# Rebuilding the opening of a one-core adaLN + attention + MLP kernel: larger loads, c turned on TensorE, one tile's LayerNorm on ScalarE, wide warm-up matmuls

## Chip, cores, metric

One core of a Trainium2 chip. The metric is device time in microseconds (us) of one execution; the span in a profile is some 1.7 us shorter. TensorE is PE in the profile (its weight loads PEld), VectorE is DVE, ScalarE is ACT, GpSimd is POOL, SyncE is SP. Most transfers are issued from SP.

## The reference, cut to what matters

```python
x = A_x                                            # 2048 x 512, bf16
mod = silu(c) @ w_mod                              # six rows of 512: sa, ca, ga, sb, cb, gb
h = layernorm(x) * (1 + ca) + sa
x = x + ga * attention(h, k_cache[-512:], v_cache[-512:], wq, wo)   # 32 heads, 8 groups, Dh 128
h = layernorm(x) * (1 + cb) + sb
x = x + gb * (relu(h @ w1) @ w2)                   # 512 -> 1792 -> 512
```

Nothing of attention can start before the first 512 rows are normalised, two of the six modulation rows are there, and both are joined in `hT`. That is the opening.

## The kernel before

Work goes in units of one head by 512 rows, 128 in all; "head n" below is unit n of these. Per unit PE does Q, scores (S), scores times v (psO) and four of the output projection's matmuls (psW), ACT the exp, DVE the division, and SP a transposing transfer that turns the head's result into `oT`. The MLP's weights lie where w_mod was and are loaded in the middle. Cuts are marked.

```python
def load_w1():                                     # w2 in the same way
    for i in range(2):
        f0, f1 = i * FC // 2, (i + 1) * FC // 2
        dma(w1_sb[:, :, f0 * P:f1 * P], w1v[:, :, f0 * P:f1 * P], f"w1{i}", writes=R_w1[f0:f1] + R_wm)
def warm(n):
    for i in range(n):
        mm(bank[WBK][:, :P], ident[:, :], ident[:, :], True, True, [R_ident], [WBK], i == n - 1)
def pv_mms(u):
    # ... psO matmuls, reciprocal and product on DVE into o_sb ...
    dma(oT[u % NOT][:, :, :], o_sb[u % NOS][:, :, :]..., transpose=True)          # on SP
def enqueue_wo(b, j):                              # four of these after each head's psO
    # ... mm(bank[WBK], oT[slot][:, tl, :], wo_sb[:, h, :], ...) ...

# opening
dma(c_col[:, :], c[0].rearrange("(c p) -> p c", p=P), "c", writes=[R_c], eng=ACT)
for t in range(TPB):
    dma(x_sb[:, t, :], xv[:, t, :], f"xa{t}", writes=[R_x[t]], eng=ACT if t % 2 else SP)
load_wm(1); load_wm(0); load_wq(0, 2); load_k(0); load_v(0); load_wq(2, 2)
# ... constants on POOL, exp table on ACT ...
warm(48)
ln_stat(0); ln_stat(1); silu(); ln_stat(2); ln_rstd(0, 0, 3); ln_stat(3); ln_rstd(0, 3, 4)
for tl in range(3):
    ln_norm(tl); ln_tposes(tl, [0, 2])
for f in mod_cols_mm(0, QBK): f()
ln_norm(3); ln_tposes(3, [0, 2]); mod_cols_evac(0, QBK)
ln_mod_ps([0, 2], hT[0], R_hT[0], 1)
# ... Q of two heads, then the loop over units ...
add(60, load_w1)                                   # at unit 60 and unit 64
add(64, load_w2)
```

Both halves of a weight claim all of `R_wm`, so SP issues the second half only when the first has landed (in the changed kernel w2's first half lands at 239.19 us and the second is issued at 239.20).

Of the kernel before, what the change touches and what calls it, by code (L numbers as in the profile page):

```python
# [7 lines left out]
ACTF = mybir.ActivationFunctionType  # L8
ALU = mybir.AluOpType
AX = mybir.AxisListType  # L10
BF = mybir.dt.bfloat16
F32 = mybir.dt.float32
# [1185 lines left out]
def build_fast(nc, es, top, A_x, A_k_cache, A_v_cache, A_wq, A_wo, B_x, B_w1, B_w2, c, w_mod, out, flag):  # L1198
    P = 128
    _, Sq, D = A_x.shape  # L1200
# [6 lines left out]
    QB = 512  # L1207
    NB = Sq // QB
    TPB = QB // P
    NT = Sq // P  # L1210
    DC = D // P
# [3 lines left out]
    scale = float(Dh) ** -0.5  # L1215
    eps = 1e-5
# [10 lines left out]
    def T(name, shape, dt=BF):  # L1227
        return es.enter_context(nc.sbuf_tensor(name, shape, dt))

    x_sb = T("x", [P, NT, D])  # L1230
# [11 lines left out]
    oT = [T(f"oT{i}", [P, TPB, P]) for i in range(NOT)]  # L1242
    acc = T("acc", [P, TPB, D], F32)
    wmw = T("wmw", [P, max(6 * DC * D, DC * F + FC * D)])
    wm = [wmw[:, i * DC * D:(i + 1) * DC * D].rearrange("p (c n) -> p c n", c=DC) for i in range(6)]
    w1_sb = wmw[:, 0:DC * F].rearrange("p (c f) -> p c f", c=DC)
    w2_sb = wmw[:, DC * F:DC * F + FC * D].rearrange("p (f d) -> p f d", f=FC)
    xn = T("xn", [P, TPB, D])
# [3 lines left out]
    yo = [PT[1][:, i, :] for i in range(NY)]  # L1252
    ident = T("ident", [P, P])
    ones = T("ones", [P, P])
    c_col = T("c_col", [P, DC])
    sc_bf = T("sc_bf", [P, DC])
    sc_rep = T("sc_rep", [P, DC, P])
    tmp = T("tmp", [P, DC], F32)
# [4 lines left out]
    mv = T("mv", [P, NT, 2], F32)  # L1263
    rstd = T("rstd", [P, NT], F32)
    cst = T("cst", [P, 4], F32)
# [9 lines left out]
    bank = [s_ps[0][:, 0, :], s_ps[0][:, 1, :], s_ps[1][:, 0, :], s_ps[1][:, 1, :], q_ps[:, :],  # L1275
            o_ps[:, 0:2, :].rearrange("p a b -> p (a b)"), o_ps[:, 2:4, :].rearrange("p a b -> p (a b)"), w_ps[:, :]]
    QBK, WBK = 4, 7

    sem = lambda name: top.enter_context(nc.semaphore(name))
    kb = KB(nc)  # L1280
    PE = kb.stream("pe", sem("s_pe"))
    ACT = kb.stream("act", sem("s_act"))
    DVE = kb.stream("dve", sem("s_dve"))
    POOL = kb.stream("pool", sem("s_pool"))
    SP = kb.stream("sp", sem("s_sp"))
# [6 lines left out]
    def dma(out_ap, in_ap, key, reads=(), writes=(), transpose=False, eng=None):  # L1292
        k = dsem(key)
        if transpose:
            return kb.op(SP, lambda e: e.dma_start_transpose(out_ap, in_ap), reads=reads, writes=writes, dma_sem=k)
        return kb.op(eng or SP, lambda e: e.dma_start(out_ap, in_ap), reads=reads, writes=writes, dma_sem=k)  # L1296

    RL = lambda name, n: [Res(f"{name}{i}") for i in range(n)]
    R_x, R_wq, R_wo = RL("x", NT), RL("wq", H), RL("wo", NPASS)
# [3 lines left out]
    R_acc, R_wm, R_w1, R_w2 = RL("acc", TPB), RL("wm", 6), RL("w1", FC), RL("w2", FC)  # L1303
    R_xn, R_xnT = RL("xn", TPB), Res("xnT")
    R_yt, R_yo = RL("yt", NY), RL("yo", NY)
    R_b = RL("bank", 8)
    R_ident, R_ones, R_c, R_sc, R_screp, R_tmp, R_cst = (Res(n) for n in ("ident", "ones", "c", "sc", "screp", "tmp", "cst"))
    R_moda, R_modb, R_ga, R_gb = Res("moda"), Res("modb"), Res("ga"), Res("gb")
    R_st, R_mv, R_rstd = RL("st", NT), RL("mv", NT), RL("rstd", NT)
    R_rinv, R_vmax, R_chk, R_good, R_flag = Res("rinv"), Res("vmax"), Res("chk"), Res("good"), Res("flag")  # L1310
    R_h1 = [RL(f"h1_{i}_", FC) for i in range(2)]

    xv = A_x[0].rearrange("(p t) d -> p t d", p=P)
# [10 lines left out]
    def load_wq(h0, n, eng=None):  # L1324
        dma(wq_sb[:, :, h0 * Dh:(h0 + n) * Dh], wqv[:, :, h0 * Dh:(h0 + n) * Dh], f"wq{h0}", writes=R_wq[h0:h0 + n], eng=eng)

    def load_k(g):
        dma(kT_sb[:, g, :], A_k_cache[0][g, Sk - W:, :], f"k{g}", writes=[R_kT[g]], transpose=True)
# [1 line left out]
    def load_v(g, eng=None):  # L1330
        dma(v_sb[:, g, :, 0:Dh], A_v_cache[0][g, Sk - W:, :].rearrange("(k p) d -> p k d", p=P), f"v{g}", writes=[R_v[g]], eng=eng)

    def load_wm(sl, eng=None):
        dma(wm[sl], w_mod[:, sl * D:(sl + 1) * D].rearrange("(c p) n -> p c n", p=P), f"wm{sl}", writes=[R_wm[sl]], eng=eng)

    def load_wo(j):
        dma(wo_sb[:, j * HQ:(j + 1) * HQ, :], wov[:, j * HQ:(j + 1) * HQ, :], f"wo{j}", writes=[R_wo[j]])
# [11 lines left out]
    def mm(out_ap, lhsT, rhs, start, stop, reads, bk, signal):  # L1349
        kb.op(PE, lambda e: e.matmul(out_ap, lhsT, rhs, start=start, stop=stop), reads=reads, group_writes=[R_b[k] for k in bk], signal=signal)  # L1350
# [3 lines left out]

    def warm(n):
        for i in range(n):
            mm(bank[WBK][:, :P], ident[:, :], ident[:, :], True, True, [R_ident], [WBK], i == n - 1)

    def ln_stat(t):
        kb.op(DVE, lambda e: e.bn_stats(st[:, t, :], x_sb[:, t, :]), reads=[R_x[t]], writes=[R_st[t]])  # L1360
        kb.op(DVE, lambda e: e.bn_aggr(mv[:, t, :], st[:, t, :]), reads=[R_st[t]], writes=[R_mv[t]])  # L1361

    def ln_rstd(b, lo=0, hi=TPB):
        sl = slice(b * TPB + lo, b * TPB + hi)
        kb.op(DVE, lambda e: e.tensor_scalar(rstd[:, sl], mv[:, sl, 1], eps, None, op0=ALU.add), reads=R_mv[sl], writes=R_rstd[sl])  # L1365
        kb.op(POOL, lambda e: e.tensor_tensor(rstd[:, sl], rstd[:, sl], cst[:, 0:1].to_broadcast([P, hi - lo]), op=ALU.pow),  # L1366
              reads=R_rstd[sl] + [R_cst], writes=R_rstd[sl])

    def ln_norm(t):
        b, tl = t // TPB, t % TPB  # L1370
        kb.op(DVE, lambda e: e.tensor_scalar(xn[:, tl, :], x_sb[:, t, :], mv[:, t, 0:1], rstd[:, t:t + 1], op0=ALU.subtract, op1=ALU.mult),  # L1371
              reads=[R_x[t], R_mv[t], R_rstd[t]], writes=[R_xn[tl]])
# [10 lines left out]
    def ln_tposes(tl, bks):  # L1383
        for cc in range(DC):
            bk = bks[cc // 2]
            o = (cc % 2) * 512 + tl * P
            tpose(bank[bk].bitcast(BF)[:, o:o + P], xn[:, tl, cc * P:(cc + 1) * P], [R_xn[tl]], [bk], cc == DC - 1)
# [15 lines left out]
    CC_ORDER = (0, 2, 1, 3)  # L1403
    QA = 2

    def silu():
        kb.op(ACT, lambda e: e.activation(tmp[:, :], c_col[:, :], ACTF.Exp, scale=-1.0), reads=[R_c], writes=[R_tmp])
        kb.op(DVE, lambda e: e.tensor_scalar(tmp[:, :], tmp[:, :], 1.0, None, op0=ALU.add), reads=[R_tmp], writes=[R_tmp])
        kb.op(DVE, lambda e: e.reciprocal(tmp[:, :], tmp[:, :]), reads=[R_tmp], writes=[R_tmp])
        kb.op(DVE, lambda e: e.tensor_tensor(sc_bf[:, :], c_col[:, :], tmp[:, :], op=ALU.mult), reads=[R_tmp, R_c], writes=[R_sc])  # L1410

    def mod_cols_mm(which, bk):
        fs = []
        for idx, sl in enumerate((0, 1) if which == 0 else (3, 4)):
            for c2 in range(DC):
                for cc in range(DC):
                    last = idx == 1 and c2 == DC - 1 and cc == DC - 1
                    fs.append(lambda sl=sl, c2=c2, cc=cc, col=idx * DC + c2, last=last: mm(
                        bank[bk][:, col:col + 1], wm[sl][:, cc, c2 * P:(c2 + 1) * P], sc_bf[:, cc:cc + 1],
                        cc == 0, cc == DC - 1, [R_sc, R_wm[sl]], [bk], last))  # L1420
        return fs

    def mod_cols_evac(which, bk):
        mo, r = which * 2 * DC, (R_moda, R_modb)[which]
        kb.op(DVE, lambda e: e.tensor_copy(modc[:, mo:mo + DC], bank[bk][:, :DC]), reads=[R_b[bk]], writes=[r])
        kb.op(DVE, lambda e: e.tensor_scalar(modc[:, mo + DC:mo + 2 * DC], bank[bk][:, DC:2 * DC], 1.0, None, op0=ALU.add), reads=[R_b[bk]], writes=[r])
# [100 lines left out]
            add(s0 + TPB + 5 + cc // 2, lambda cc=cc: ln_mod_sb(cc, dst, r, which))  # L1527


    dma(c_col[:, :], c[0].rearrange("(c p) -> p c", p=P), "c", writes=[R_c], eng=ACT)  # L1530
    for t in range(TPB):
        dma(x_sb[:, t, :], xv[:, t, :], f"xa{t}", writes=[R_x[t]], eng=ACT if t % 2 else SP)
    load_wm(1)
    load_wm(0)
    load_wq(0, 2)
    load_k(0)
    load_v(0)
    load_wq(2, 2)
    kb.op(POOL, lambda e: e.memset(ones[:, :], 1.0), writes=[R_ones])
    kb.op(POOL, lambda e: e.affine_select(ident[:, :], ones[:, :], pattern=[[1, P]], compare_op=ALU.is_equal, fill=0.0,  # L1540
                                          base=0, channel_multiplier=-1), reads=[R_ones], writes=[R_ident])
    kb.op(POOL, lambda e: e.memset(cst[:, 0:1], -0.5), writes=[R_cst])
    kb.op(POOL, lambda e: e.memset(v_sb[:, :, :, P:VW], 1.0), writes=[R_v1])
    kb.op(ACT, lambda e: e.activation(cst[:, 2:3], cst[:, 0:1], ACTF.Exp), reads=[R_cst], writes=[Res("dummy")])
    warm(48)
    ln_stat(0)
    ln_stat(1)
    silu()
    ln_stat(2)
    ln_rstd(0, 0, 3)  # L1550
    ln_stat(3)
    ln_rstd(0, 3, 4)
    for tl in range(3):
        ln_norm(tl)
        ln_tposes(tl, [0, 2])
    for f in mod_cols_mm(0, QBK):
        f()
    ln_norm(3)
    ln_tposes(3, [0, 2])
    mod_cols_evac(0, QBK)  # L1560
    ln_mod_ps([0, 2], hT[0], R_hT[0], 1)
    load_wq(R, R)
    load_k(1)
# [8 lines left out]
    for g in range(G):  # L1572
        for i, op in enumerate((ALU.max, ALU.min)):
            add(max(R * g, 3), lambda g=g, i=i, op=op: kb.op(DVE, lambda e: e.tensor_reduce(vmax[:, i, g:g + 1], v_sb[:, g, :, 0:Dh], axis=AX.XY, op=op),
                                                             reads=[R_v[g]], writes=[R_vmax]))
# [221 lines left out]
```

## Time and profile before

| | before |
|---|---|
| time, three runs | 569.95 to 571.03, median 570.52 us |
| span of the profiled run | 568.2 us |
| PE busy | 553.0 us, 97% |
| half clock | about 9.4 to 16.2 us |
| first score matmul | 16.26 us |

A number such as 16.26 is a start in the timeline, from the start of the span.

### The profile page before, as it was taken

Reading aid. Unit: us, or ns where it says so; the run is one execution under the profiler, and the core shown is the slowest. Engines: PE = TensorE matmul, PEld = TensorE weight load, DVE = VectorE, ACT = ScalarE, POOL = GpSimd, SP = SyncE. Lnnn points to the kernel's source line nnn. Section 1 sums busy time; section 2 is a strip of 40 time slices with the busy share of each in tenths; the row PEclk is TensorE's granted clock in tenths of the full one; section 3 lists DMA queues with packets and bytes.
Section 4 is the critical chain, followed back from the end, with each engine's and each line's share of the span. In section 5 each row is a group of like instructions: output and inputs, shape, how many; then the busy total and the mean of one; then the engine's idle time right before and its main releaser. Section 6 shows DMA issues by size and latency. Waiting matters only on the chain.

```text
span 568.2 us, 9662 instructions
## 1 busy us (share of the span) xinstructions
PE 553.0 (97%) x4094; PEld 318.7 (56%) x4169; DVE 242.9 (43%) x532; ACT 347.3 (61%) x445; POOL 38.7 (7%) x41
## 2 busy tenths in 40 slices
PE   6999999999999999989999999999999999999997
PEld 5565555666655555546666555555555654444443
DVE  4344465533334655323336553333354438322133
ACT  2876666666666666656666666666666654432500
POOL 1000000002300000023000000330000000000000
PEclk8999999999999999999999999999999999999999
DMA  8795768331231145742321432121114220210001
GB/s 227 202 192 119 179 131 171 81 74 38 39 76 38 38 81 124 167 108 42 75 39 37 75 75 39 38 38 38 38 37 67 47 39 1 38 38 22 22 28 47
DMA packets 111620, 42.67 MB, mean 75 GB/s; under 512 B 94032, under 2 KB 111184, under 8 KB 111568
## 3 DMA queue, kind: packets, MB, share of 16 engines
q1 hardware_dynamic: 110752, 41.70, 34.4%
q8 instruction: 34, 0.56, 0.4%
q10 hardware_dynamic: 816, 0.26, 0.2%
q14 instruction: 18, 0.15, 0.1%
HBM read 18.35 MB, written 2.10 MB: 36 GB/s over the span
## 4 chain that ended last, share of the span: by engine, by line
PE 96%; DMA 2%; DVE 1%; issue 1%; ACTq 0%
PE psS L1350 28%; PE psO L1350 26%; PE psQ L1350 23%; PE psW L1350 19%; DMA oT<-o 1%; DMA x<-in_A_x_dram 1%; DVE st L1360 0%; PE psS L1353 0%; DVE hT L1397 0%; DVE PT L1631 0%; DVE PT L1632 0%; DVE mv L1361 0%; DVE o L1475 0%; ACTq L1296 0%; DVE xn L1371 0%
## 5 line engine op out<-in xcount | busy, mean ns | idle before, releaser
L1464 ACT ACTIVATE PT<-psS 128x1024 bf16<-128x1024 f32 x256 | 262.8, 1028 | 131.7 <-PE psS L1350 131.7
L1350 PE MATMUL psS<-qT,kT 128*128 128x512 bf16 x509 | 151.2, 379 | 0.2
L1350 PEld LDWEIGHTS psO<-v,PT 128*128 128x128 bf16 x2048 | 126.6, 98 | 30.2
L1350 PE MATMUL psO<-v,PT 128*128 128x129 bf16 x2048 | 137.0, 220 | 0.0
L1350 PE MATMUL psQ<-hT,wq 128*128 128x512 bf16 x507 | 130.8, 381 | 1.1 <-DVE hT L1397 1.1
L1474 DVE RECIPROCAL rinv<-psO 128x4 f32<-128x4 f32 x128 | 23.3, 182 | 234.5 <-PE psO L1350 234.5
L1350 PE MATMUL psW<-wo,oT 128*128 128x512 bf16 x451 | 118.1, 379 | 5.3 <-DMA oT<-o 2.1
L1475 DVE TENSOR_TENSOR o<-psO,rinv 128x512 bf16<-128x512 f32 x128 | 88.5, 691 | 4.7 <-DVE rinv L1474 0.3
L1350 PEld LDWEIGHTS psQ<-hT,wq 128*128 128x128 bf16 x508 | 49.7, 98 | 61.1 <-issue 1.0
L1350 PEld LDWEIGHTS psS<-qT,kT 128*128 128x128 bf16 x512 | 49.7, 98 | 59.5 <-ACT PT L1464 0.7
L1456 ACT ACTIVATE qT<-psQ 128x512 bf16<-128x512 f32 x127 | 75.4, 593 | 1.2 <-PE psQ L1350 1.2
L1350 PEld LDWEIGHTS psW<-wo,oT 128*128 128x128 bf16 x512 | 44.9, 98 | 35.4 <-DMA oT<-o 2.6
L1620 ACT ACTIVATE wq<-psS 128x512 bf16<-128x512 f32 x56 | 33.4, 597 | 49.2 <-PE psS L1350 49.2
L1497 DVE TENSOR_TENSOR acc<-psW,acc 128x512 f32<-128x512 f32 x48 | 33.1, 690 | 9.0 <-PE psW L1350 9.0
L1350 PE MATMUL psO<-wmw,wq 128*128 128x512 bf16 x136 | 31.0, 379 | 0.3
L1366 POOL TENSOR_TENSOR rstd<-rstd,cst 128x4 f32<-128x4 f32 (+2 forms) x9 | 8.6, 961 | 273.5 <-DVE rstd L1365 273.4
L1500 POOL TENSOR_TENSOR acc<-acc,gaf 128x512 f32<-128x512 f32 x12 | 15.2, 1268 | 171.0 <-DVE acc L1497 171.0
L1350 PE MATMUL psS<-h2T,wmw 128*128 128x512 bf16 x110 | 25.2, 379 | 0.1
L1350 PE MATMUL psS<-hT,wmw 128*128 128x512 bf16 x110 | 24.4, 379 | 0.1
L1631 DVE TENSOR_TENSOR PT<-psO,gbf 128x512 f32<-128x512 f32 x10 | 6.9, 691 | 40.2 <-PE psO L1350 40.2
L1360 DVE BATCH_NORM_STATS2 st<-x 128x6 f32<-128x512 bf16 x32 | 21.7, 680 | 4.6 <-DMA x<-in_A_x_dram 4.6
L1350 PEld LDWEIGHTS psO<-wmw,wq 128*128 128x128 bf16 x140 | 13.7, 98 | 16.5
(60 smaller groups left out, 168.8 us busy)
## 6 DMA issues: line engine op xcount, KB each, us to landing
wo<-in_A_wo_dram SPq DMA_DIRECT2D x4, 1024.0 KB, 5.9
wq<-in_A_wq_dram SPq DMA_DIRECT2D x7, 512.0 KB, 5.8
wmw<-in_B_w_dram SPq DMA_DIRECT2D x4, 896.0 KB, 5.2
wmw<-in_w_mod_dram SPq DMA_DIRECT2D x6, 512.0 KB, 5.2
oT<-o SPq DMA_TRANSPOSE x128, 2.4
out_dram<-PT SPq DMA_DIRECT2D x16, 128.0 KB, 1.7
x<-in_A_x_dram SPq DMA_DIRECT2D x3, 512.0 KB, 4.2
v<-in_A_v_cache_dram SPq DMA_DIRECT2D x8, 128.0 KB, 4.6
```

The source lines that it names most:

```text
L1350: kb.op(PE, lambda e: e.matmul(out_ap, lhsT, rhs, start=start, stop=stop), reads=reads, group_writes=[R_b[k] for k in bk], signal=signal)
L1360: kb.op(DVE, lambda e: e.bn_stats(st[:, t, :], x_sb[:, t, :]), reads=[R_x[t]], writes=[R_st[t]])
L1366: kb.op(POOL, lambda e: e.tensor_tensor(rstd[:, sl], rstd[:, sl], cst[:, 0:1].to_broadcast([P, hi - lo]), op=ALU.pow), reads=R_rstd[sl] + ...
L1456: kb.op(ACT, lambda e: e.activation(qT[u % NQT][:, :], bank[bk], ACTF.Copy), reads=[R_b[bk]], writes=[R_qT[u % NQT]])
L1464: kb.op(ACT, lambda e: e.activation(PT[u % NPT][:, pr * 2:pr * 2 + 2, :], s_ps[pr][:, :, :], ACTF.Exp, scale=scale), reads=[R_b[pr * 2], R ...
L1474: kb.op(DVE, lambda e: e.reciprocal(rinv[:, u, :], o_ps[:, :, P]), reads=[R_b[5], R_b[6]], writes=[R_rinv])
L1475: kb.op(DVE, lambda e: e.tensor_tensor(o_sb[u % NOS][:, :, :], o_ps[:, :, 0:P], rinv[:, u, :].unsqueeze(2).to_broadcast([P, TPB, P]), op=A ...
L1497: kb.op(DVE, lambda e: e.tensor_tensor(acc[:, tl, :], bank[WBK], acc[:, tl, :], op=ALU.add), reads=[R_b[WBK], R_acc[tl]], writes=[R_acc[tl]])
L1500: kb.op(eng, lambda e: e.tensor_tensor(acc[:, tl, :], acc[:, tl, :], gaf[:, :], op=ALU.mult), reads=[R_acc[tl], R_ga], writes=[R_acc[tl]])
L1620: kb.op(ACT, lambda e: e.activation(h1T[b % 2][:, fc, :], bank[bk], ACTF.Relu), reads=[R_b[bk]], writes=[R_h1[b % 2][fc]], pre=all_events( ...
L1631: kb.op(DVE, lambda e: e.tensor_tensor(yt[i], bank[bk], gbf[:, :], op=ALU.mult), reads=[R_b[bk], R_gb], writes=[R_yt[i]], pre=pt_done if c ...
```

## The change

The intent: shorten the time to the first score, and keep PE's clock up on the way. The diff, cut to its core:

```diff
-    wm = [... one transfer for each of slices 0 and 1 ...]
+    # slices 0 and 1 lie side by side, two transfers of 2 KB rows, each half of the contraction
-            mm(bank[WBK][:, :P], ident[:, :], ident[:, :], True, True, [R_ident], ...)
+            mm(bank[WBK], ones[:, :], ones[:, 0:1].to_broadcast([P, QB]), True, True, [R_ones], ...)
-    dma(c_col[:, :], c[0].rearrange("(c p) -> p c", p=P), "c", ..., eng=ACT)
-    for t in range(TPB):
-        dma(x_sb[:, t, :], xv[:, t, :], f"xa{t}", ..., eng=ACT if t % 2 else SP)
+    dma(c_row[:, :], c[0].rearrange("(c p) -> c p", p=P), "c", ..., eng=ACT)
+    for i in range(2):
+        dma(x_sb[:, 2 * i:2 * i + 2, :], xv[:, 2 * i:2 * i + 2, :], f"xa{i}", ..., eng=ACT if i else SP)
-    warm(48)
+    warm(5); silu_exp(5)          # c transposed on PE, exp read from PSUM
+    warm(14)
+    # tile 3 on ACT: Copy with sum, mean, Square with sum, variance, later the normalising Identity
-    ln_stat(0); ln_stat(1); silu(); ln_stat(2); ...; ln_stat(3); ...
+    ln_stat(0); ln_stat(1); rstd(0:2); ln_stat(2); rstd(2:4); silu_mul(5); ln_norm(0..2)
-    # transposes of tiles 0 to 2, all modulation columns, transposes of tile 3
+    # half the columns, tile 0, the other half, then tiles 1, 2, 3 followed by warm(1), warm(2), warm(3)
```

Nothing after the first Q matmul is touched.

More of the change, by code (lines that the diff above doesn't have):

```diff
@@ L1244, in build_fast @@
     wmw = T("wmw", [P, max(6 * DC * D, DC * F + FC * D)])
-    wm = [wmw[:, i * DC * D:(i + 1) * DC * D].rearrange("p (c n) -> p c n", c=DC) for i in range(6)]
+    wm01 = wmw[:, 0:2 * DC * D].rearrange("p (c n) -> p c n", c=DC)
+    wm = [wm01[:, :, 0:D], wm01[:, :, D:2 * D]] + [wmw[:, i * DC * D:(i + 1) * DC * D].rearrange("p (c n) -> p c n", c=DC) for i in range(2, 6)]
     w1_sb = wmw[:, 0:DC * F].rearrange("p (c f) -> p c f", c=DC)
@@ L1254, in build_fast @@
     ones = T("ones", [P, P])
-    c_col = T("c_col", [P, DC])
+    c_row = T("c_row", [DC, P])
+    s3 = T("s3", [P, 4], F32)
     sc_bf = T("sc_bf", [P, DC])
@@ L1309, in build_fast @@
     R_st, R_mv, R_rstd = RL("st", NT), RL("mv", NT), RL("rstd", NT)
+    R_s3, R_eps = Res("s3"), Res("eps")
     R_rinv, R_vmax, R_chk, R_good, R_flag = Res("rinv"), Res("vmax"), Res("chk"), Res("good"), Res("flag")
@@ L1331, in load_v, with load_wm, load_wm01, wm_res @@
         dma(v_sb[:, g, :, 0:Dh], A_v_cache[0][g, Sk - W:, :].rearrange("(k p) d -> p k d", p=P), f"v{g}", writes=[R_v[g]], eng=eng)
-    def load_wm(sl, eng=None):
-        dma(wm[sl], w_mod[:, sl * D:(sl + 1) * D].rearrange("(c p) n -> p c n", p=P), f"wm{sl}", writes=[R_wm[sl]], eng=eng)
+    def load_wm(sl):
+        dma(wm[sl], w_mod[:, sl * D:(sl + 1) * D].rearrange("(c p) n -> p c n", p=P), f"wm{sl}", writes=[R_wm[sl]])
+    wm01v = w_mod[:, 0:2 * D].rearrange("(c p) n -> p c n", p=P)
+    def load_wm01(i):
+        c0, c1 = i * DC // 2, (i + 1) * DC // 2
+        dma(wm01[:, c0:c1, :], wm01v[:, c0:c1, :], f"wm{i}", writes=[R_wm[i]])
+    def wm_res(sl, cc):
+        return R_wm[cc // (DC // 2)] if sl < 2 else R_wm[sl]
     def load_wo(j):
@@ L1356, in warm @@
         for i in range(n):
-            mm(bank[WBK][:, :P], ident[:, :], ident[:, :], True, True, [R_ident], [WBK], i == n - 1)
+            mm(bank[WBK], ones[:, :], ones[:, 0:1].to_broadcast([P, QB]), True, True, [R_ones], [WBK], i == n - 1)
     def ln_stat(t):
@@ L1404, in build_fast, with silu_exp, silu_mul @@
     QA = 2
-    def silu():
-        kb.op(ACT, lambda e: e.activation(tmp[:, :], c_col[:, :], ACTF.Exp, scale=-1.0), reads=[R_c], writes=[R_tmp])
+    def silu_exp(bk):
+        cT = bank[bk].bitcast(BF)[:, 0:DC]
+        kb.op(PE, lambda e: e.transpose(cT, c_row[:, :], ident[0:DC, 0:DC]), reads=[R_c, R_ident], group_writes=[R_b[bk]])
+        kb.op(ACT, lambda e: e.activation(tmp[:, :], cT, ACTF.Exp, scale=-1.0), reads=[R_b[bk]], writes=[R_tmp])
+    def silu_mul(bk):
+        cT = bank[bk].bitcast(BF)[:, 0:DC]
         kb.op(DVE, lambda e: e.tensor_scalar(tmp[:, :], tmp[:, :], 1.0, None, op0=ALU.add), reads=[R_tmp], writes=[R_tmp])
         kb.op(DVE, lambda e: e.reciprocal(tmp[:, :], tmp[:, :]), reads=[R_tmp], writes=[R_tmp])
-        kb.op(DVE, lambda e: e.tensor_tensor(sc_bf[:, :], c_col[:, :], tmp[:, :], op=ALU.mult), reads=[R_tmp, R_c], writes=[R_sc])
+        kb.op(DVE, lambda e: e.tensor_tensor(sc_bf[:, :], cT, tmp[:, :], op=ALU.mult), reads=[R_tmp, R_b[bk]], writes=[R_sc])
     def mod_cols_mm(which, bk):
@@ L1419, in mod_cols_mm @@
                         bank[bk][:, col:col + 1], wm[sl][:, cc, c2 * P:(c2 + 1) * P], sc_bf[:, cc:cc + 1],
-                        cc == 0, cc == DC - 1, [R_sc, R_wm[sl]], [bk], last))
+                        cc == 0, cc == DC - 1, [R_sc, wm_res(sl, cc)], [bk], last))
         return fs
@@ L1527, in add_ln @@
             add(s0 + TPB + 5 + cc // 2, lambda cc=cc: ln_mod_sb(cc, dst, r, which))
-    dma(c_col[:, :], c[0].rearrange("(c p) -> p c", p=P), "c", writes=[R_c], eng=ACT)
-    for t in range(TPB):
-        dma(x_sb[:, t, :], xv[:, t, :], f"xa{t}", writes=[R_x[t]], eng=ACT if t % 2 else SP)
-    load_wm(1)
-    load_wm(0)
+    dma(c_row[:, :], c[0].rearrange("(c p) -> c p", p=P), "c", writes=[R_c], eng=ACT)
+    for i in range(2):
+        dma(x_sb[:, 2 * i:2 * i + 2, :], xv[:, 2 * i:2 * i + 2, :], f"xa{i}", writes=R_x[2 * i:2 * i + 2], eng=ACT if i else SP)
@@ L1535, in build_fast @@
+    load_wm01(0)
+    load_wm01(1)
     load_wq(0, 2)
+    load_wq(2, 2)
     load_k(0)
     load_v(0)
-    load_wq(2, 2)
     kb.op(POOL, lambda e: e.memset(ones[:, :], 1.0), writes=[R_ones])
+    kb.op(POOL, lambda e: e.memset(cst[:, 0:1], -0.5), writes=[R_cst])
     kb.op(POOL, lambda e: e.affine_select(ident[:, :], ones[:, :], pattern=[[1, P]], compare_op=ALU.is_equal, fill=0.0,
                                           base=0, channel_multiplier=-1), reads=[R_ones], writes=[R_ident])
-    kb.op(POOL, lambda e: e.memset(cst[:, 0:1], -0.5), writes=[R_cst])
+    kb.op(POOL, lambda e: e.memset(cst[:, 1:2], eps), writes=[R_eps])
@@ L1543, in build_fast @@
     kb.op(POOL, lambda e: e.memset(v_sb[:, :, :, P:VW], 1.0), writes=[R_v1])
     kb.op(ACT, lambda e: e.activation(cst[:, 2:3], cst[:, 0:1], ACTF.Exp), reads=[R_cst], writes=[Res("dummy")])
-    warm(48)
+    warm(5)
+    silu_exp(5)
+    warm(14)
+    t3 = TPB - 1
+    kb.op(ACT, lambda e: e.activation(xn[:, t3, :], x_sb[:, t3, :], ACTF.Copy, accum_out=s3[:, 0:1]), reads=[R_x[t3]], writes=[R_xn[t3], R_s3])
+    kb.op(ACT, lambda e: e.activation(s3[:, 1:2], s3[:, 0:1], ACTF.Copy, scale=-1.0 / D), reads=[R_s3], writes=[R_s3])
@@ new lines, in build_fast, with rstd_add @@
+    kb.op(ACT, lambda e: e.activation(xn[:, t3, :], x_sb[:, t3, :], ACTF.Square, bias=s3[:, 1:2], accum_out=s3[:, 2:3]), reads=[R_x[t3], R_s3], writes=[R_xn[t3], R_s3])
+    kb.op(ACT, lambda e: e.activation(rstd[:, t3:t3 + 1], s3[:, 2:3], ACTF.Identity, scale=1.0 / D, bias=cst[:, 1:2]), reads=[R_s3, R_eps], writes=[R_rstd[t3]])
+    def rstd_add(lo, hi):
+        kb.op(DVE, lambda e: e.tensor_scalar(rstd[:, lo:hi], mv[:, lo:hi, 1], eps, None, op0=ALU.add), reads=R_mv[lo:hi], writes=R_rstd[lo:hi])
@@ L1546, in build_fast, with rstd_pow @@
+    def rstd_pow(lo, hi):
+        kb.op(POOL, lambda e: e.tensor_tensor(rstd[:, lo:hi], rstd[:, lo:hi], cst[:, 0:1].to_broadcast([P, hi - lo]), op=ALU.pow),
+              reads=R_rstd[lo:hi] + [R_cst], writes=R_rstd[lo:hi])
     ln_stat(0)
     ln_stat(1)
-    silu()
+    rstd_add(0, 2)
+    rstd_pow(0, 2)
     ln_stat(2)
-    ln_rstd(0, 0, 3)
-    ln_stat(3)
-    ln_rstd(0, 3, 4)
+    rstd_add(2, 3)
+    rstd_pow(2, 4)
+    silu_mul(5)
     for tl in range(3):
         ln_norm(tl)
-        ln_tposes(tl, [0, 2])
@@ L1556, in build_fast @@
-    for f in mod_cols_mm(0, QBK):
-        f()
-    ln_norm(3)
-    ln_tposes(3, [0, 2])
-    mod_cols_evac(0, QBK)
+    kb.op(ACT, lambda e: e.activation(s3[:, 3:4], s3[:, 1:2], ACTF.Copy, scale=rstd[:, t3:t3 + 1]), reads=[R_s3, R_rstd[t3]], writes=[R_s3])
+    kb.op(ACT, lambda e: e.activation(xn[:, t3, :], x_sb[:, t3, :], ACTF.Identity, scale=rstd[:, t3:t3 + 1], bias=s3[:, 3:4]),
+          reads=[R_x[t3], R_rstd[t3], R_s3], writes=[R_xn[t3]])
+    fs = mod_cols_mm(0, QBK)
+    for f in fs[:len(fs) // 2]:
+        f()
@@ L1561, in build_fast @@
+    ln_tposes(0, [0, 2])
+    for f in fs[len(fs) // 2:]:
+        f()
+    mod_cols_evac(0, QBK)
+    for tl in range(1, TPB):
+        ln_tposes(tl, [0, 2])
+        warm(tl)
     ln_mod_ps([0, 2], hT[0], R_hT[0], 1)
```

## The prediction

> **What bounds the kernel now.** I read the page first: the shares of the engines, then the line of the granted clock.
>
> ```profile
> span 568.2 us, 9662 instructions
> PE 553.0 (97%) x4094; PEld 318.7 (56%) x4169; DVE 242.9 (43%) x532; ACT 347.3 (61%) x445; POOL 38.7 (7%) x41
> ...
> PEclk8999999999999999999999999999999999999999
> ...
> PE 96%; DMA 2%; DVE 1%; issue 1%; ACTq 0%
> ```
>
> TensorE is busy for 97% of the span and makes up 96% of the chain that ended last. The change touches only what runs before attention. So it can win only what PE loses in the opening: the one slice (14 us each) whose PE digit is 6 and whose clock digit is 8. Everything later is PE at full clock, and I expect it to move earlier as a block.
>
> Next I cut the opening into stretches by what PE does, and read busy time and granted clock in each (columns: window, length, busy us and number of instructions for PE, PEld, DVE, ACT and POOL, clock, DMA share, GB/s).
>
> ```profile
> 1.40:6.43 5.03, 5.02 (x48) 4.85 (x48) 1.72 (x5) 1.69 (x3) 0.24 (x1) 1.00 0.64 183
> 6.43:9.40 2.97, 0.00 (x0) 0.00 (x0) 2.76 (x12) 0.00 (x0) 1.24 (x2) 1.00 1.22 342
> 9.40:12.20 2.80, 2.74 (x48) 2.48 (x48) 1.25 (x5) 0.00 (x0) 0.32 (x1) 0.50 1.22 239
> 12.20:16.26 4.06, 2.98 (x8) 1.24 (x10) 1.33 (x3) 2.04 (x3) 0.00 (x0) 0.50 1.15 326
> 16.26:20.00 3.74, 3.74 (x20) 1.44 (x19) 0.00 (x0) 3.54 (x5) 0.00 (x0) 1.00 1.07 287
> ```
>
> The 48 warm-up matmuls end at 6.43, PE idles 2.97 us, and from about 9.4 to 16.2 the clock is half: transposes, modulation columns and the first eight Q matmuls all run cold. (The 1.00 of the first row is before the first recorded change at 5.97; 48 matmuls of 128 columns in 5.02 us are 105 ns each, so they ran cold as well.)
>
> Then the chain that ended last, and the timeline, for why PE idled (start, length, what).
>
> ```profile
> 1.27 4.25 DMA x<-in_A_x_dram
> ...
> 5.55 0.70 DVE st L1360
> ...
> 8.94 0.42 DVE xn L1371
> 9.37 0.05 issue
> 9.41 1.46 PE psS L1353 x12
> 10.87 0.83 PE psQ L1350 x32
> 11.71 0.46 PE psS L1353 x4
> 12.17 0.04 issue
> 12.21 1.01 DVE hT L1397 x2
> 13.22 0.06 issue
> 13.28 1.49 PE psQ L1350 x3
> 14.77 1.65 PE psO L1350 x4
> ```
>
> VectorE waited until 5.53 for the second tile of x, then did three tiles' statistics and the silu in one queue; PE got its first xn at 9.41. The packets of the trace say why that tile was late: it sits on the ACT queue behind c, which came in as 512 packets of 2 bytes from 2.19 to 3.95 us; x's packets on that queue start only at 4.06. Meanwhile SP's 1 KB packets crawl too: from 2.5 to 4.0 the rate is 67 GB/s, from 6 to 8 it is 380. Landings from issue times plus time to landing: x tiles 3.3, 5.5, 4.75 and 7.0; c 4.4; w_mod's two slices 7.8 and 9.3; first wq 10.1; first kT 10.8; first v 11.3.
>
> [...]its clock changes lie 3.413 and 6.827 us apart (5.97, 9.38, 16.2). [...]the window 9.4 to 12.8, mostly transposes and one-column matmuls, did not lift the clock, and the next one of wide matmuls did. [...]the trace has 597 ns for the 512-column copy and about 720 ns with two pointers[...].
>
> **The change part by part.**
> *c as 4 rows.* 512 packets become 4. By the first packet's 2.19 and the half microsecond or so from x's last packet to its landing, I put c at about 2.9 instead of 4.4, and some 1.7 us of crawling DMA is gone. It costs one small PE transpose.
> *2 KB rows.* x comes in two transfers of 256 KB, w_mod's first 1 MB in two halves by contraction rows. At 380 GB/s from about 2 us: first x pair about 3.5, second about 4.5, w_mod (1.57 MB in all) about 6.7 instead of 9.3, wq 7.5 and 9, kT and v about 10. I take all these off the path.
> *VectorE queue.* Three statistics (0.69 + 0.18 each) instead of four, silu after them. From 3.5: two tiles to 5.3, rstd add 5.5, third tile and its add 6.6, silu (0.14 + 0.18 + 0.16 and gaps) 7.15, two norms (0.40 each) 7.95, third 8.35.
> *Tile 3 on ACT.* Copy with sum 0.6, small op 0.2, [...]small op 0.2, and about 0.2 for each of two accumulator reads (my guess): with gaps 2.3 us from 4.5, so 6.8; the POOL power 0.86 to 7.75; small op and normalise 0.2 + 0.75 to about 8.8. PE wants it at about 10, so a microsecond is spare.
> *Wide warm matmuls.* They start when `ones` is set (0.98) and not after the last constant (1.41). Five at the cold spacing of 0.427 (the psO Q matmuls) end at 3.2; c's transpose to 3.4; then fourteen. If the clock rises at 5.97 as before, six run cold and eight at 0.215 (0.86 per four later in the chain): end at 7.7. There is then no idle stretch of 3 us, so no return to half clock.
> *PE after that, at full clock.* 16 columns 0.47 (32 took 0.94 at full clock near 32 us), 8.2; four transposes 0.25 (half of the cold 0.49), 8.45; 16 columns 8.9; transposes and fill of one, two and three wide matmuls: 9.15, 9.4, 9.6, 10.05, 10.3; fill to 10.95. hT can start at 10.5, against 12.2: 1.7 us.
> *hT and Q.* VectorE 0.5 each to 11.0 and 11.5, ACT 0.72 each to 11.2 and 11.95. Q of head 0: matmuls at 11.05, 11.27, 11.55, 12.0, the last waiting for ACT, end 12.2; head 1, four at 0.215, to 13.07. Its qT for head 0 is ready at 13.0. The first score matmul starts at about 13.1 instead of 16.26. From hT that is 2.6 us in place of 4.06, so 1.5 us from the clock.
> Sum: 1.7 + 1.5 = 3.2 us. Everything from the first score on is the same program at the same clock, so 570.5 - 3.2 = 567.3.
>
> **Rivals.**
> *The PE fill itself becomes the bound.* 19 wide matmuls are fixed work ahead of the modulation columns in PE's queue. The phase of the clock's window is not the kernel's: if the clock rises at 4.4, the fill ends near 6.8 and silu's 7.15 is the wait; if at 7.8, it ends near 8.5. That moves the gain between about 2.4 and 4. [...]
> *ACT or the transfers end last.* If the second x pair lands at 6, tile 3 is ready near 10.3, and hT slips to about 10.7: gain 3.0. If accumulator reads cost far more than I guess, the same. If a second table load (1.28 us in this trace) were needed for Square, gain 2 to 2.5.
> *The gain is given back.* The first heads alternate between PE and ACT (S, exp, Q), so an earlier start could run into wq, kT or v of the second key group. DMA is at 240 to 350 GB/s until 20 us and idle from 20 to 23, ahead of a need at about 17, so I count nothing for it. If it did: 568.5 to 570.
> *More gain.* If runs of the old kernel often had worse clock phases than the profiled one (569.93, the lowest of its times), the gain over the median is up to 4.5: 566.
>
> **Range and chances.** The timed runs of before spread over 1.1 us[...]; my steps are good to about a microsecond. Range 565.9 to 568.8. A 2% change would need 11.4 us, nearly all of the 13 us before the first Q matmul, so "within 2%" is close to certain; a little is left for slower, should some load or wait go wrong.
>
> **What would show it.** In the profile of after: no 2-byte packets; c and x in by 3 and 4.5 us; PE never idle for over a microsecond after 1.1 us; clock full from its first rise; transposes of tile 3 ending near 10.3; hT at 10.5 and the first score matmul at 13.1, with the span near 565. Wrong if: the clock falls again, wide matmuls still run cold past 8 us, the last hT waits for ACT's xn, or the scores start by 13.1 but the span is not 3 us shorter.

The forecast's sum came to 1.7 + 1.5 = 3.2 us, from 570.5 to 567.3. Cut are passages that no trace or run of this case shows: general statements on the clock, on c's packets and on the cost of an ACT instruction, one step of ACT's tile, a rival in which c comes late, and a reading of the scatter of before. ACT's Square is in the 2.3 us of that tile, which is off the forecast's path (0.72 us in the profile after). The other ACT steps rest on the trace of before: 0.60 us for a copy of 512 columns, 1.45 for the two hT with two pointers each, 0.20 for a small op. The changes at 5.97, 9.38 and 16.2 are those of the granted clock in the trace of before (5.99, 9.41 and 16.23 by the timeline's zero); of the two windows after 9.4, PE was busy for 2.74 us of 3.40 in the one with the transposes and 2.92 in the other. "No idle stretch of 3 us, so no return to half clock" rests on one case, the 2.97 us without a matmul before the fall at 9.4. On the phase of the windows see "When the clock falls".

## More of the kernel before

The lines themselves stand in the prediction. One line matters that it does not show, from the list of who waited for whom on PE (engine, line, what for: us in total, times, longest), cut to 200 to 300 us:

```profile
PE psW L1350 <- DMA oT<-o: 2.1, 1, 2.1
```

PE, the bound, waits once in the middle of the kernel for a turned head.

## The result, and the profile after

The changed kernel took 569.87 us (median of four, 568.60 to 570.62), the old one 570.59 in the same rounds. The ratio is 0.9986, interval 0.9963 to 1.0009: no difference. (A ratio here is the mean of one kernel's fast runs over the mean of the other's of the same rounds, so not quite the ratio of the medians.) It lies within 2%, as forecast, but outside the stated range of 565.9 to 568.8.

The page of the changed kernel, the lines that answer to those of before:

```profile
span 568.7 us, 9702 instructions
PE 560.5 (99%) x4147; PEld 316.4 (56%) x4147; DVE 241.7 (42%) x529; ACT 350.7 (62%) x453; POOL 38.6 (7%) x42
PEclk9999999999999999989999999999999999999999
```

The dent in the clock has gone from the first slice, as wanted. A new one stands in the 18th, near 245 us, in code that nobody changed.

**The opening did gain.** The chain that ended last, in the opening (start, length, what):

```profile
1.71 6.75 DMA wmw<-in_w_mod_dram
...
8.50 0.50 PE psQ L1362 x14
...
11.18 0.65 PE psW L1362 x3
...
13.11 0.86 PE psO L1362 x4
13.97 0.51 PE psS L1362 x2
```

The Q matmuls run at 0.215 us each (0.86 for four). The first score matmul starts at 13.88 us in the timeline, 2.38 earlier than before. What the opening waits for now is w_mod's second half, which landed at 8.46.

**Where it went.** I matched the 256 exps on ACT one by one between the two traces and listed where the difference in start changes:

| event | after minus before, us | step |
|---|---|---|
| first exp | -2.44 | the opening |
| every exp to the end of head 66 | -2.44 | |
| first exp of head 67, near 245 us | -1.64 | +0.80 |
| first exp of head 68 | +0.03 | +1.67 |
| all other exps, and the MLP to 520 us | +0.02 | |
| MLP from 523 us | +0.53 | +0.50 |

The whole gain is lost within 7 us. The chain at that place, old kernel, then changed one:

```profile
240.61 0.51 DVE o L1475
241.11 5.47 DMA oT<-o
246.59 0.05 issue
246.63 0.39 PE psW L1350
```

```profile
231.89 1.95 SPq L1297
233.85 0.04 issue
233.89 5.30 DMA wmw<-in_B_w_dram
239.19 0.02 issue
239.20 0.37 SPq L1298
239.62 5.33 DMA oT<-o
244.95 0.05 issue
244.99 0.39 PE psW L1362
245.38 0.43 PE psS L1362 x2
245.81 1.53 PE psQ L1362 x4
```

In both, a turned head lands some 5.4 us after its issue (5.47 and 5.33; the median of all 128 is 2.4 in either trace), with 896 KB of w2 queued ahead of it. In the changed kernel the chain goes further back: SP's first half of w2 was issued late, since the transposing transfer before it (head 62's) took 1.95 us to issue. Then four Q matmuls take 1.53 in place of 0.86. The stretches around the wait (columns as in the prediction) show why:

```profile
238.60:242.06 3.46, 3.46 (x28) 1.89 (x26) 0.84 (x3) 2.43 (x3) 0.00 (x0) 1.00 0.41 93
242.06:244.99 2.93, 0.00 (x0) 0.00 (x1) 0.30 (x1) 0.00 (x0) 0.00 (x0) 1.00 1.14 312
244.99:249.28 4.29, 4.29 (x21) 2.42 (x22) 0.69 (x1) 2.64 (x3) 2.41 (x2) 0.60 0.09 18
```

PE idles 2.93 us, and the clock is 0.60 on average for the next 4.29: the trace has half clock from 245.87 to 249.28, one window of 3.413 us, which costs 1.67. The old kernel kept its clock at the same place, during its wait and after it:

```profile
244.50:246.63 2.13, 0.00 (x0) 0.00 (x0) 0.29 (x1) 0.00 (x0) 0.00 (x0) 1.00 1.22 291
246.63:250.00 3.37, 3.31 (x27) 2.06 (x29) 0.96 (x3) 2.43 (x3) 2.09 (x2) 1.00 0.07 13
```

The last +0.50 is the weight load after the branch of PE's program near 522 us, which waited 0.41 us in one trace and 0.91 in the other ("issue", no releaser). Over all twelve later profiles that step lies between 0 and 0.5 in kernels of both families, so I count it as scatter.

### The profile page after: what moved, and what is told of

Its sections match the earlier page's. It is cut to its first block, busy times and chain, and to the rows that moved or that the text cites. A ratio compares the mean times of both kernels' runs of the same rounds, so it can differ in the third digit from the quotient of the medians.

```text
span 568.7 us, 9702 instructions
## 1 busy us (share of the span) xinstructions
PE 560.5 (99%) x4147; PEld 316.4 (56%) x4147; DVE 241.7 (42%) x529; ACT 350.7 (62%) x453; POOL 38.6 (7%) x42
## 4 chain that ended last, share of the span: by engine, by line
PE 95%; DMA 3%; SPq 1%; DVE 0%; issue 0%
PE psS L1362 28%; PE psO L1362 26%; PE psQ L1362 22%; PE psW L1362 20%; DMA wmw<-in_w_mod_dram 1%; DMA oT<-o 1%; DMA wmw<-in_B_w_dram 1%; SPq L1297 0%; SPq L1298 0%; PE psS L1365 0%; DVE PT L1672 0%; DVE o L1492 0%; DVE PT L1673 0%; DVE rinv L1491 0%
## 5 line engine op out<-in xcount | busy, mean ns | idle before, releaser
L1362 PE MATMUL psW<-wo,oT 128*128 128x512 bf16 x512 | 130.8, 379 | 2.9 <-DMA oT<-o 2.9
L1378 POOL TENSOR_TENSOR rstd<-rstd,cst 128x4 f32<-128x4 f32 x7 | 7.1, 1011 | 264.7 <-DVE rstd L1377 264.7
```

Of the source, the lines that this page charges most:

```text
L1362: kb.op(PE, lambda e: e.matmul(out_ap, lhsT, rhs, start=start, stop=stop), reads=reads, group_writes=[R_b[k] for k in bk], signal=signal)
L1378: kb.op(POOL, lambda e: e.tensor_tensor(rstd[:, sl], rstd[:, sl], cst[:, 0:1].to_broadcast([P, hi - lo]), op=ALU.pow), reads=R_rstd[sl] + ...
```

## The experiments

My theory: the opening's gain is real and travels unharmed to unit 66. There the wait behind the MLP loads and the return to half clock eat it. Rivals: the later part has a pace of its own and would give back any gain; or the first profile was chance. Groups 1 and 2 (four kernels each) ran on one chip, group 3 on another; kernels are compared within a group. Mean clock tells the half-clock time of a run: one window of 3.413 us in 568 makes 0.997, two 0.994, three 0.991. It does not tell where a window lies: before_spread, with no wait in the middle, has 0.991 from its opening alone (10.24 us of half clock there), and the 0.999 of after_fill below is half clock in the last 1.5 us of its span.

### Group 1: repeat both kernels, and take the wait away from both

*after_again* and *before_again* are the two kernels unaltered.

> The changed kernel once more, unaltered. My theory: the opening gains 2.4 us in every run (first score matmul near 13.9 us), and what takes it back is in the middle: TensorE waits about 2.9 us near 242 us for one head's turned output (oT), whose transfer stands behind the loads of the MLP weights, and where the clock's window falls badly it then runs 3.4 us at half clock, 1.7 us more. So runs whose mean clock is 1.00 should have spans near 567, and runs with 0.997 near 568.5. Rival (chance): the first profile was an outlier, the median is 567 to 568 and no stall of over 2.2 us is seen.

Measured: 571.94 us (569.91 to 572.23), ratio 1.0024 to the old kernel. First exp -2.67 against the first profile of before; wait 2.86; then half clock; at the end -0.06. The clocks of its runs were 0.993 to 0.997, none 1.00. Three of the five (0.993 and 0.994) had some two windows' worth and spans of 570.2 to 570.5, above the 568.5 that I expected; the profiled run is not one of them, so where their second window lies is not known. So not chance: if anything the change loses.

> The old kernel once more, unaltered, for a second profile. My theory: first score matmul at 15 to 16.5 us depending on the phase of the clock's window, a stall of 2 to 3 us near 244 us for oT, the span 568 to 569.5. Rival (chance): the stall differs by over 1 us from that of the first profile, 2.1 us.

Measured: one look, 571.51 us. Wait 2.45 us, and this time half clock after it too (247.7 to 251.1), which cost 1.66 us. The old kernel can fall there as well.

*before_spread* and *after_spread* carry the same edit:

```diff
-    def load_w1():
-        for i in range(2):
-            f0, f1 = i * FC // 2, (i + 1) * FC // 2
+    def load_w1(i):
+            f0, f1 = i * FC // 4, (i + 1) * FC // 4        # w2 the same
-    add(60, load_w1)
-    add(64, load_w2)
+    for i in range(4):
+        add(60 + 2 * i, lambda i=i: load_w1(i))
+        add(68 + 2 * i, lambda i=i: load_w2(i))
```

> The old kernel with the MLP weights loaded in eight pieces of 448 KB, two heads apart, in place of four of 896 KB in two pairs. My theory: the stall of 2.1 us near 244 us goes, nothing else changes: span 566.1, time about 2 us under the kernel before (568.4). Rival (the later part has a pace of its own, set by ACT or by transfers): the wait reappears elsewhere and the time stays within 0.5 us of before.

> The changed kernel with the same eight pieces. My theory: no stall, no return to half clock in the middle, and so the whole 2.4 us of the opening reaches the end: span 564.0 to 564.5, time 565.7 to 566.2, 2.0 to 2.5 us under the old kernel with the same pieces. Rival (a pace of its own): within 1 us of the old kernel with the same pieces.

Measured: before_spread 568.51 us (567.41 to 569.02), after_spread 565.90 (565.46 to 566.45). Both times lie where the theory put them. The profiled spans, 567.3 and 564.7, lie above the expected 566.1 and 564.0 to 564.5: before_spread had one more cold window in its opening than the first profile of before. The means of the times differ by 2.43 us. All of PE's waits over 0.15 us in the two profiles, before_spread first:

```profile
PE psS L1351 <- DVE xn L1369: 3.5, 1, 3.5
PE psW L1348 <- POOL cst L1540: 1.4, 1, 1.4
PE psQ L1348 <- DVE hT L1395: 1.1, 1, 1.1
```

```profile
PE psQ L1360 <- DVE sc_bf L1425: 1.2, 1, 1.2
PE psW L1360 <- POOL cst L1555: 1.0, 1, 1.0
PE psS L1363 <- DVE xn L1381: 0.4, 1, 0.4
```

No line with oT is left, and all five runs of after_spread have clock 1.00. The opening's gain reaches the end once the middle has no wait. A pace of its own is ruled out.

### Group 2: the half clock, the slow issue, the warm-up

*after_control* is the changed kernel a third time.

> The changed kernel a third time, as the control of the next two. My theory: one transposing transfer on the SP queue, head 62's, takes 1.8 to 2.0 us to issue (1.19 us for most heads and in the old kernel), the MLP load behind it starts later by that, and the wait for oT near 242 us is 2.9 us. In nearly all runs the clock then falls to half for one or two windows of 3.4 us. Time 569.5 to 572. Rival (chance): stall and slow issue differ from the two earlier profiles of it by over 0.5 us.

Measured: 569.77 us (569.38 to 571.27). Head 62's issue 2.06 us, wait 3.00. This profile differs in two ways. No half clock came after the wait. And the opening gained nothing: first exp +0.31, because the second x pair landed at 8.49 us in place of 6.55, silu stands behind that pair's statistics in DVE's queue, PE waited 3.1 us for it, and the clock fell in the opening (11.1 to 14.5).

*after_fill* puts work into the wait:

```diff
+        if s == 66:
+            pop_bg(3)
+            for i in range(10):
+                mm(bank[QBK], ones[:, :], ones[:, 0:1].to_broadcast([P, QB]), True, True, [R_ones], [QBK], i == 9)
+            pop_bg(1)
```

> The changed kernel with ten wide matmuls on ones put in TensorE's queue just ahead of the matmul that waits for oT near 242 us, into the Q bank, whose value has been read by then: 2.15 us of filler inside the wait. My theory (the loss there is the wait plus a return to half clock): the wait ends at the same moment, PE idles 0.8 us, the clock stays full to the end, and the time is 1.7 us or more under the control. Rival (the half clock costs nothing, because something else has a pace there): the clock stays full and the time is within 0.7 us of the control.

Measured: 568.74 us, 1.03 under the control by the medians, and clocks 0.999 or 1.00 in all five runs. The stretch of the fill and the one after it:

```profile
242.00:244.15 2.15, 2.15 (x10) 0.78 (x8) 0.27 (x1) 0.00 (x0) 0.00 (x0) 1.00 1.16 341
244.15:245.02 0.87, 0.00 (x1) 0.01 (x1) 0.00 (x0) 0.00 (x0) 0.00 (x0) 1.00 1.28 228
```

The wait ends at 245.02, as in the changed kernel's first profile (244.99), and the only loss is +0.92. The half clock is thus a cost of its own, and here ten useless matmuls removed it. The 1.7 us I expected against the control is not reached, because not every run of the control fell there: one has clock 1.00, and the profiled one lost its clock in the opening instead.

*after_xsp* issues the second x pair on SP (`eng=SP` for both).

> The changed kernel with the second x pair issued on SP ahead of w_mod, not on ACT. My theory of the slow issue (it falls at a fixed place in SP's sequence, which the change moved by issuing fewer transfers there): with one transfer more on SP the slow issue leaves head 62 (or moves to an earlier head) and the wait near 242 us is 2.1 to 2.5 us again, as in the old kernel. Rival: head 62 is slow again, the wait 2.9 us. For the opening: x tiles 2 and 3 land near 5.3 us and not 6.5, w_mod as before at 8.5; the last normalised tile is ready about a microsecond earlier, and the first score comes 0.3 to 0.4 us earlier, near 13.5; if the transfers' slow start is what counts, no gain.

Measured: 569.64 us (568.23 to 571.26). Head 62 was slow again (2.06 us, wait 2.95), so my first idea, a fixed place in SP's sequence, fell. In the opening x landed at 4.60, but w_mod at 9.12, and the first score came at 14.35, later than I expected: what x gained w_mod lost.

*before_wide* changes the old kernel's warm-up alone, to `warm(21)` with the changed kernel's wide matmul.

> The old kernel with 21 warm-up matmuls of 512 columns on ones in place of 48 of 128 columns on the identity, nothing else. My theory: PE is busy until the first xn at 9.4 us, the clock never falls in the opening, and the first score matmul comes at about 14.2 us, that is 2.1 of the rebuilt opening's 2.4 us from this one part. The middle is as in the old kernel (wait 2.1 to 2.5 us, half clock afterwards in a few runs). Time 568.4 to 569. Rival (the earlier data are what counts): first score at 15.5 us or later, time 570 or more.

Measured: 572.71 us, slower than before (ratio 1.0034). First score at 15.68. The clock fell all the same, at 12.27. The window just before it, and the next:

```profile
8.86:12.27 3.41, 2.07 (x48) 1.70 (x48) 2.31 (x8) 0.66 (x1) 0.69 (x1) 1.00 1.30 248
12.27:15.68 3.41, 2.99 (x8) 1.27 (x10) 0.68 (x2) 1.38 (x3) 0.00 (x0) 0.50 1.16 321
```

PE looks busy for 2.07 of 3.41 us there, with 16 transposes and 32 one-column matmuls, and this did not hold the clock; which of the two kinds did not was not separated. Wide warm-up alone thus didn't hold it: first score and time are those of the rival, not mine. The changed kernel has six wide fillers among these transposes and held it (1.00 from 6.93 to 245.87 us in its first profile); that they are the reason was not isolated. In the middle the wait was 3.8 us, the longest of all. That set me looking at what collides with these transfers.

### Group 3: the length of PE's program

The packets of the traces hold an answer. The instruction queue moves one packet of 16 KB about every 16 us, after every 250 or so of PE's matmuls and weight loads, and one takes 0.88 us or more. (Between 40 and 500 us the counts are 228 to 299 in the old kernel, median 255, and 228 to 275 in the changed one, median 260; where two packets lie 24.1 and 28.5 us apart in the old kernel, they are 249 and 261. From this I take the packets for fetches of PE's program.) In the profiles of kernels with the changed opening from groups 1 and 2, and in the first one, one of these starts 0.28 to 0.44 us into head 62's issue. In the old kernel it falls at 232.2, between head 61's issue (ended 232.0) and head 62's (234.3). The changed opening has 74 matmuls where the old one had 96, so each later fetch comes later in the work by 22 matmuls and their weight loads: this one starts 43 of PE's records ahead of head 62's issue in the old kernel's trace and 4 after it in the changed one's. In before_wide, 27 matmuls shorter than before, the packet fell into w2's first half instead, which took 6.75 us to land (5.1 before). Two kernels test this from both sides:

```diff
 # after_pad
-    warm(14)
+    warm(7)                                    # and 29 of 128 columns
 # before_less: same columns in 26 matmuls
-    warm(48)                                   # of 128 columns
+    warm(26)                                   # of 236 columns
```

> The changed kernel with the fill of 14 wide matmuls made of 7 wide and 29 of 128 columns: the same columns within 2%, and 22 matmuls more, so that TensorE's program is as long up to any later point as the old kernel's. My theory: the slow issue of head 62's transfer comes from a 16 KB packet of the instruction queue (TensorE fetches its program every 250 matmuls and weight loads or so), which in the changed kernel starts 0.4 us into that issue and in the old one falls between two transfers. With the length restored the packet misses: head 62 issues in 1.19 us, the wait near 242 us is 2.1 to 2.5 us, the clock stays full there in most runs, and the median time is 568 to 569.3. Rival (the slow issue belongs to the changed kernel's time line, not to the length of its program): head 62 takes 1.8 us or more again, wait 2.9 to 3.0, time 569.7 or more.

> The old kernel with its 48 warm-up matmuls of 128 columns replaced by 26 of 236 columns: the same columns, 22 matmuls fewer, so that its program is as long as the changed kernel's. My theory: the fetch now falls into head 62's issue (1.8 us or more), the wait near 244 us grows from 2.1-2.5 to 2.9-3.1, most runs go to half clock there, and the time is 1 to 2.5 us over the kernel before. Rival: head 62 at 1.19, wait and time as before.

Head 62's transfer in the timeline of SP (start, length, ...), in the old, the changed, after_pad and before_less:

```profile
234.33 1.19 SPq L1295 DMA_TRANSPOSE oT<-o  x1
```

```profile
231.89 1.95 SPq L1297 DMA_TRANSPOSE oT<-o  x1
```

```profile
232.55 1.19 SPq L1297 DMA_TRANSPOSE oT<-o  x1
```

```profile
235.37 1.72 SPq L1295 DMA_TRANSPOSE oT<-o  x1
```

The waits of PE that follow are 2.1, 2.9, 2.1 and 2.8 us. In before_less a fetch packet starts 0.36 us into the issue, in after_pad none starts in it. The slow issue goes and comes with the number of matmuls in the opening: shown from both sides. The other heads agree. In the 14 profiles, 35 issues of a turned head (seven different heads, ten profiles) have such a packet starting 0.2 to 0.67 us into them, and all 35 took 1.62 to 2.87 us; 129 have one starting 0.85 to 1.19 us into them, and none took more than 1.20; between 0.67 and 0.85 both occur (2.11 us at 0.72 and 1.20 at 0.71 in the old kernel's first profile). A fetch is not the only cause of a slow issue: head 56 took 1.68 to 1.75 in all 14 profiles with no such packet in it. Times: after_pad 570.13 us (567.13 to 570.75), ratio 0.997 to the old kernel of its group (571.10); before_less 572.03, ratio 1.0023. The time of after_pad missed my range, and that of before_less, 0.93 us over the old kernel by the medians, lies just under mine. In the profile of before_less no half clock followed the wait, against what I expected; its 0.991 is three cold windows in the opening (8.3 to 18.5 us), so its time is not the price of the longer wait alone. Four of its six runs still had one window at half clock (0.997; in the profiled one it followed the wait), and two had none (567.13 and 568.33). On this chip the old kernel had three windows' worth (0.990 or 0.991) in 8 of 11 runs, against one of nine in group 1; the mean does not say whether these lie in the opening or the middle.

*after_ccol* loads c as before, as 512 packets of 2 bytes.

> The changed kernel with c loaded as the old one does, 512 packets of 2 bytes on the ACT queue, and no transpose of c. My theory (those packets hold up the data behind them): the second x pair, behind c on ACT, lands about 1 us later than in the changed kernel (6.3 to 8.5), so 7.5 to 9, w_mod 9 to 9.5, and the first score comes 0.8 to 1.5 us later than the same run would have it, at 15 us or more. Rival (the transfers start slowly anyway): x and w_mod land within 0.3 us of the changed kernel's best (6.5 and 8.5), first score by 14.2.

Measured: one look, 570.40 us. The second x pair landed at 8.20, w_mod at 9.03, first exp -0.79, first score 15.53. All three lie where my theory put them, but also inside what kernels with the changed loading of c showed (6.32 to 8.49 for that pair, 7.88 to 9.40 for w_mod, up to 16.63 for the first score), so what c's packets cost stays open.

*after_spread_xsp* joins two edits.

> The changed kernel with the MLP weights in eight pieces and the second x pair on SP. My theory: no wait in the middle, and an opening whose silu no longer waits for a late x: the first score at 14.0 to 14.5 in every run in place of 13.6 to 16.5, so time 565.3 to 566 with a smaller spread than the 1.0 us of the eight pieces alone (565.5 to 566.5). Rival: w_mod, now behind all of x, costs as much as x gains, and the median is within 0.3 us of 565.9 with the same spread.

Measured: 565.57 us (565.30 to 566.05), first score at 14.00 in the one profile, ratio 0.9905; after_spread had 0.9918 in its own group, and the intervals overlap (0.9891 to 0.9919, 0.9905 to 0.9932). It is 5.5 us under the old kernel of its group (571.10). after_spread was 4.7 under the old kernel (570.58) and 6.0 under the changed one (571.94) in its group. Either beats both kernels; that after_spread_xsp beats after_spread is not shown.

### When the clock falls

Eleven profiles have the wait near 245 us. I laid the clock's windows (3.413 us, counted on from each trace's first recorded change) over it, and took the larger share of one window in which PE idled. (In the first profiles of both kernels the changes inside the span lie 1.00 and 2.00 of these windows apart in the old one, at 5.99, 9.41 and 16.23 us, and 70.00 and 1.00 in the changed one, at 6.93, 245.87 and 249.28. Their phase is not the kernel's: the falls at 9.41 and 247.7 in the two profiles of the old kernel are 69.8 windows apart, those at 245.87 and 11.1 in after and after_control 68.8.)

| profile | wait, us | largest idle share of one window | fell to half |
|---|---|---|---|
| after_fill | 0.87 | 19% | no |
| before_less | 2.83 | 49% | no |
| before | 2.14 | 50% | no |
| after_control | 3.00 | 53% | no |
| after_ccol | 3.15 | 55% | no |
| after_pad | 2.08 | 61% | yes |
| after_again | 2.86 | 64% | yes |
| before_again | 2.45 | 66% | yes |
| after | 2.94 | 74% | yes |
| after_xsp | 2.95 | 81% | yes |
| before_wide | 3.80 | 98% | yes |

The share sorts them without an exception; the length of the wait alone doesn't. A fall cost 1.67 us in after and 1.66 in before_again. The openings of the 14 profiles fit the same line: five windows with 70 to 87% of idle time were followed by half clock, and full-clock windows with at most 49% were not, with one exception, the 39% of before_wide's window of transposes. That a share between 55 and 61% is the border was found by sorting, and no run was made to test it.

## Why the prediction was wrong

- *PE at full clock bounds the kernel, the opening has the only dent.* Right for the span as a whole. I read the clock in tenths of 14 us slices and passed over the one wait in the middle.
- *"Everything from the first score on is the same program at the same clock."* This is the step that failed. The program is the same, but its clock and its waits are not. It cost 0.80 (longer wait) and 1.67 us (half clock) of the first profile's 2.44. The smaller opening alone would not have sufficed: 570.5 less 2.44 is 568.1, inside the range.
- *The rival "the gain is given back"* was named, but I looked for it within the first 30 us alone, at the loads of the second key group. It came at 245 us, at the loads of the MLP.
- *The size of the opening, 3.2 us.* The mechanism was right, the size not: 2.38 measured (2.44 by the first exp), and in the other profiles with this opening, by the first exp, from 2.67 to none. The mis-sized term is the transfers. I took 380 GB/s from 2 us on; the packets show 156 to 254, by half microseconds, until 3.5 us in the changed kernel (312 to 389 from there to 8.5), although c's small packets were gone, so c was at most a part of the slow start. x landed at 4.28 and 6.55 (said 3.5 and 4.5), w_mod at 8.46 (said 6.7). The 1 us of slack that I gave ACT's tile was used up: its transposes started at 10.78, not 10. x's second pair on the ACT queue landed at 6.3 to 8.5 us beside SP's w_mod, and at 4.60 when SP issued it ahead of w_mod (after_xsp).
- *The wide warm matmuls.* Right that the clock holds; their end came near 8.2 us, with w_mod and silu, as the rival "PE fill" had it, and not at 7.7.
- *ACT's tile, table load.* Right: the accumulator reads took 0.19 us each (guessed 0.2), and no second table load appears.
- *What would make it wrong.* The first score at 13.9 with a span that is not shorter: close to the last clause of the prediction.

What stays open: how much c's 2-byte packets cost; why half clock was more frequent in the old kernel on one chip than on the other (the phase of the windows is not the kernel's, as the falls listed above show); and why a fetch packet that starts in a transfer's issue slows it, as only the coincidence and its removal are shown, and what makes other issues, like head 56's, slow without one.

## What to carry to other kernels

When a change shortens the front of a kernel that one engine bounds, go through the list of that engine's waits to the end of the kernel before counting the gain: here a wait of 2.14 us became one of 2.94 and a window of 3.41 us at half clock. Put bulk loads in pieces between the small transfers that the bound engine waits for; here that alone was worth 2 us (570.58 to 568.51), and it let the opening's 2.4 us through. If a wait cannot be removed, try useless wide matmuls in it: ten of them kept the clock here (0.999 or 1.00 in all five runs of after_fill).
